# A three-stage kernel on one core: a new written-out order of all steps, other engines for many small steps, and three hand-overs that wait for all readers

## The chip, the cores and the metric

The kernel runs on one NeuronCore of a Trainium2 chip. The metric is the device time of one execution in microseconds (us). The program uses five engines side by side: TensorE (PE, matrix products into PSUM), VectorE (DVE), ScalarE (ACT), GpSimd (POOL, which doesn't reach PSUM here), and SyncE (SP), whose queue issues most transfers. Each engine runs its own list of instructions strictly in order and waits on semaphores for the others.

## The reference, cut to what matters

Three layers follow each other, on 4 batches of 768 positions and 320 channels, all in f32:

```
for t in range(768):                       # mLSTM, 8 heads of 40
    m_new = maximum(f[t] + m, i[t]);  f_s = exp(f[t] + m - m_new);  i_s = exp(i[t] - m_new)
    C = f_s * C + i_s * outer(v[t], k[t]);  n = f_s * n + i_s * k[t]
    y[t] = sigmoid(o[t]) * (C @ q[t]) / maximum(abs(n @ q[t]), 1)

h = relu(x @ w_in);  u, v = h[:, :512], h[:, 512:]       # gMLP
v_n = (v - mean(v)) / sqrt(var(v) + 1e-6)
x = (u * (w_spatial @ v_n + b_spatial)) @ w_out

for e in range(4):                         # attention experts, two of four chosen per position
    a = softmax(causal(0.125 * (x @ wq[e]) @ (x @ wk[e]).T))
    out += chosen_weight(e) * (a @ (x @ wv[e])) @ wo[e]
```

## The kernel before, in words

Each batch is cut into 6 blocks of 128 positions, 24 blocks n in all; gMLP and the q/k/v products work on units of up to 3 blocks (9 units). Precision comes from splitting: a f32 operand becomes a high f16 half (a cast, on ACT, DVE or POOL) and a low half (operand less high half, one subtraction with two inputs on DVE or POOL), and a product is made of three f16 products. Only the first 6 blocks (NF=6) multiply decay weights and values in f32.

The mLSTM is computed block by block. Names in the order are thread names with a number. PL loads q/k, v/o gates and the gate rows (SP). PD and FH make the decay matrix (PE, then exp on ACT, then a causal mask on POOL). PM and FS scale q/k and split them into stacks `qs` (strings qks, qkh, qkl), transposed by a DMA on SP into `qkT`. FW multiplies q by k and by the decay. PV and FP split the values (wf, wh, wl, vh, vl). FM updates the state and splits it (cm, ch, cl). PM goes on with the numerator, the division and the gate (exd, y), splits the result (x1h, x1l) and transposes it into `x1T`. PN normalises a block for the gMLP, with a power of -0.5 on POOL; PU and FG are the gMLP; PQ, FQ, FV and FO make q, k, v and the choice of experts; PA, FE and FZ are attention, where rows `ahl` are transposed by SP into `aT` and results `os` into `oT`, and PA stores them (string res casts the result out of PSUM). PI, PS, PW, PO and PR load and split the weights (PS the spatial ones), their loads issued from ACT's queue; PG and FT prepare the gates, FU sends their rounded pieces to DRAM.

Each thread is a Python generator that yields between steps: the engine of its next step, the buffers it needs, and the events it waits for. `ORDER` (line 348) is a written-out list of thread names, 3,108 of them: `Flow.run` (line 292) takes one name after the other and lets that thread do its next step. So the list fixes the order of instructions on every engine. `CFG` (line 312) holds a string per kind of step, one letter per instance (a ACT, v DVE, p POOL, - none). `_cost` (line 44) and `charge` keep bookkeeping times; they matter here only in that a buffer is taken in the order of the times at which its copies came free (`buffers`, line 265). All matmul and vector calls pass through one helper (line 145), hence L145 in nearly every row of the profile.

Hand-overs that the change touches: in `gates` (from line 560) a f32 tile is rounded to three bf16 pieces in turn, pieces 0 and 2 sharing a buffer, and `send` (line 631) copies each to DRAM; in `mlstm` the step x1l ends with the return of the block's v/o buffer; in `gmlp` the last unit of a batch returns the batch's normalised tiles.

Of the kernel before, what the change touches and what calls it, by code (L numbers as in the profile page):

```python
# [363 lines left out]
PV4 PV5 PM4 PM3 PK3 PN2 PM3 PV4 PT5 PL5 PM3 PV5 PN2 PK3 PM3 PN2 PN2 PM3 PM3 PN2 FM5 FM4 PM3 PN2 PN2 PD5 FH10 FH11 PM4
FH10 FM4 PM3 PD5 PU0 FH11 PM4 PK4 FH10 PN2 PL6 FH11 FM4 PM4 PM6 PN2 FM4 PM6 FW10 FS12 FW11 PM4 FM4 PK4 PU0 FG0 FS13
FW11 FW10 PN3 FG0 PM4 PK4 PT6 PL6 PV6 PM4 PT6 FS13 PM5 PV6 FP6 PM4 FS12 PN3 PM4 PM4 PN3 FP6 PM6 PN3 PM4 PN3 PN3 PD6
FH12 PV6 PN3 FG0 PN3 PM5 PV6 FH12 FG0 PM4 PN3 FH13 FH12 PM5 FG0 FH13 PL7 PD6 PN3 FW12 FH13 FG1 FW12 PM5 PV6 FW12 FW13
PM5 PN4 FG1 PM5 FW12 PM5 FW13 PM5 FW13 PL7 PM7 FM6 FR6 PN4 PM7 PM5 FW13 FG2 PM5 FM6 FS15 PM5 PN4 PN4 PM6 FM6 FG2 FG3
PM5 PN4 PM6 FS15 FS14 FM6 PN4 PT7 PL7 FG1 PM6 PV7 FS14 PU0 FG2 PV7 FP7 PM6 FG1 PN4 PT7 PM7 PN4 FP7 PM6 FG3 PD7 FH14
FH15 PX0 PX0 PM6 FH14 FG2 PV7 FH15 PD7 PN5 PN4 FH14 PV7 PN4 FH15 PL8 PV7 FG3 PM6 PN5 PU1 FG2 PN5 FG3 PN5 PM6 PM6 FM7  # L370
PM6 PN5 FW14 FW15 FW14 FG3 FM7 PM6 FG2 FW15 FW14 FG3 PN5 FM7 FW15 FG2 FW14 PM8 PL8 FM7 PM8 FG3 FS17 FW15 FG1 FM7 FS16
PM7 PN5 FS17 PN5 PN6 FR7 FS16 PM8 PN5 PN5 PM7 PT8 FG2 PN6 PM7 FG3 PT8 FG2 PV8 FG0 PN6 PM7 FG2 PN6 PL8 FG3 PV8 FP8 FG1
PM7 PL9 FG3 FG2 FG0 PM7 PN6 FG3 FG2 PM7 FG1 FP8 PD8 FH16 FH17 PN6 FH16 FG1 FG3 FH17 PD8 FG0 PM7 PN6 PN6 FG1 FG4 FG1
FH17 PM7 PM7 PN6 FH16 FG1 FG0 FG1 PM7 FG5 PN6 PM9 FG0 PM7 PV8 PM9 FW16 FG4 FW17 FG5 FS19 FW16 FG6 FG0 PL9 FW17 PV8
FS18 FG0 PV8 FW16 FG7 FW17 FG6 FS18 FW16 FM8 FW17 PU1 PN7 PU0 FG7 FM8 FR8 FS19 PT9 PL9 PV9 PT9 FM8 PM9 PU0 PM8 PV9 FM8
PN7 PD9 FH18 FM8 FH19 PM8 FH18 PN7 PD9 FG6 FH19 PM8 FH18 PN7 FH19 FP9 PL10 PM8 PN7 PM8 PN7 PM8 PM8 FP9 PN7 PM8 PN7
FW18 FW19 FG6 PV9 PN7 FG7 FW18 PM8 FW19 FW18 PM8 PN7 PV9 FW19 PM10 PV9 FW18 FW19 FM9 PM8 PM9 PM10 FS20 FS21 FS21 PM8
# [1139 lines left out]
```

## Time and profile before

| | |
|---|---|
| median of 3 runs (lowest to highest) | 592.48 us (589.35 to 596.07) |
| the profiled execution: span from its first to its last instruction | 589.3 us; the fastest of the runs took 589.35 us |
| instructions | 14241 |
| mean granted TensorE clock | 0.984 of full speed |

The profile is of one execution. A busy share is an average over stages with different limits, and an idle engine costs nothing unless what it does next is waited for. PE's ends are modelled, so its busy time is an upper bound of its work. In the chain of waits, time is put down to an engine only while the chain ran through it; "DMA" there is a transfer that was waited for.

### The profile page before, as it was taken

Reading aid. Unit: us, or ns where it says so; the run is one execution under the profiler, and the core shown is the slowest. Engines: PE = TensorE matmul, PEld = TensorE weight load, DVE = VectorE, ACT = ScalarE, POOL = GpSimd, SP = SyncE. Lnnn points to the kernel's source line nnn. Section 1 sums busy time; section 2 is a strip of 40 time slices with the busy share of each in tenths; the row PEclk is TensorE's granted clock in tenths of the full one; section 3 lists DMA queues with packets and bytes.
Section 4 is the critical chain, followed back from the end, with each engine's and each line's share of the span. In section 5 each row is a group of like instructions: output and inputs, shape, how many; then the busy total and the mean of one; then the engine's idle time right before and its main releaser. Section 6 shows DMA issues by size and latency. Waiting matters only on the chain.

```text
span 589.3 us, 14241 instructions
## 1 busy us (share of the span) xinstructions
PE 484.1 (82%) x5384; PEld 344.4 (58%) x5384; DVE 483.2 (82%) x1253; ACT 345.3 (59%) x823; POOL 183.1 (31%) x306
## 2 busy tenths in 40 slices
PE   1104588899989888999989998999898999987984
PEld 0004556555646547576665665666475768776773
DVE  7899977868887788989899877999987886658883
ACT  3454446677555587657757447763737643217785
POOL 3022557575564134333324552244310000000000
PEclk9999999999997999999999998999999999999999
DMA  6768583545452879969679687548865855346820
GB/s 191 201 210 203 123 197 72 129 83 112 76 135 58 170 156 177 178 127 151 143 172 186 114 183 132 126 65 158 141 131 128 161 121 85 80 101 116 163 66 23
DMA packets 179404, 78.73 MB, mean 134 GB/s; under 512 B 160198, under 2 KB 168456, under 8 KB 179336
## 3 DMA queue, kind: packets, MB, share of 16 engines
q1 hardware_dynamic: 173552, 69.04, 59.2%
q10 hardware_dynamic: 5784, 8.79, 5.1%
q8 instruction: 42, 0.69, 0.5%
q14 instruction: 26, 0.21, 0.1%
HBM read 25.31 MB, written 4.52 MB: 51 GB/s over the span
## 4 chain that ended last, share of the span: by engine, by line
PE 32%; DVE 28%; DMA 15%; ACT 11%; issue 6%; POOL 5%; SPq 3%; ACTq 0%; DVEq 0%; POOLq 0%
PE g L145 30%; SPq L145 3%; DMA rows<-r_dram 3%; DVE ahl L145 3%; DVE sm L145 3%; DVE g L145 3%; DMA oT<-os 3%; DMA aT<-ahl 2%; PE pst L145 2%; DMA qkT<-qs 2%; ACT pst L145 2%; DVE qs L145 2%; DVE u L145 2%; DVE aT L145 2%; ACT ahl L145 2%
## 5 line engine op out<-in xcount | busy, mean ns | idle before, releaser
L145 PE MATMUL g<-wsT,vn 128*128 128x384 f16 (+2 forms) x612 | 93.4, 307 | 0.1
L145 PEld LDWEIGHTS <-vn 128*128 128x128 f16 x648 | 59.7, 98 | 31.4 <-issue 0.6
L145 PEld LDWEIGHTS <-qkst 128*128 128x128 f16 x424 | 35.5, 100 | 28.1 <-issue 9.3
L145 PE MATMUL g<-gT,w_h 128*128 128x384 f16 (+2 forms) x288 | 49.1, 315 | 2.1 <-DVE ahl L145 2.1
L145 ACT ACTIVATE pst<-pst,sm 128x640 f32<-128x640 f32 (+1 forms) x32 | 26.5, 830 | 37.5 <-DVE sm L145 37.5
L145 PE MATMUL g<-qkst 128*128 128x384 f16 (+4 forms) x224 | 37.7, 298 | 8.8 <-DVE ahl L145 5.6
L145 POOL TENSOR_SCALAR_AFFINE_SELECT dd<-dd 128x512 f32<-128x512 f32 x48 | 31.0, 666 | 44.6 <-ACT dd L145 44.5
L145 ACT ACTIVATE dd<-g 128x512 f32<-128x512 f32 x48 | 26.3, 598 | 20.4 <-PE g L145 20.3
L145 PEld LDWEIGHTS <-w_h 128*128 128x128 f16 x288 | 27.2, 100 | 16.8 <-issue 3.9
L145 ACT ACTIVATE g<-g,sm 128x256 f32<-128x256 f32 (+3 forms) x64 | 32.4, 510 | 6.5 <-DVE sm L145 6.1
L145 PE MATMUL g<-vv,aT 128*128 128x64 f16 x1008 | 33.8, 193 | 2.8 <-DVE sm L145 0.9
L145 PE MATMUL g<-wi_h,x1T 128*128 128x512 f16 x120 | 31.7, 397 | 4.0 <-DMA x1T<-xs 2.0
L145 PEld LDWEIGHTS <-aT 128*128 128x128 f16 x1008 | 32.2, 98 | 4.8 <-issue 3.0
L145 DVE TENSOR_REDUCE sm<-g 128x1 f32<-128x256 f32 (+3 forms) x64 | 29.0, 479 | 5.7 <-PE g L145 5.5
L145 PE MATMUL g<-x1T,wi_h 128*128 128x384 f16 (+2 forms) x180 | 31.9, 308 | 1.5 <-DVE ahl L145 0.8
L145 DVE TENSOR_TENSOR ahl<-pst,ahl 128x640 f16<-128x640 f32 (+1 forms) x32 | 28.3, 883 | 5.6 <-ACT ahl L145 5.0
L145 PEld LDWEIGHTS <-x1T 128*128 128x128 f16 x192 | 18.3, 100 | 24.9 <-issue 4.2
L145 PEld LDWEIGHTS <-qkT 80*128 80x128 f16 (+1 forms) x512 | 24.2, 100 | 12.9 <-DMA qkT<-qs 6.7
L145 DVE TENSOR_REDUCE sm<-pst 128x1 f32<-128x640 f32 (+1 forms) x32 | 28.2, 882 | 3.5 <-PE pst L145 3.2
L145 POOL TENSOR_TENSOR nt<-nt,mhalf 128x1 f32<-128x1 f32 x24 | 15.4, 642 | 49.5 <-DVE nt L145 38.6
L145 DVE TENSOR_TENSOR ahl<-g,ahl 128x128 f16<-128x128 f32 (+3 forms) x64 | 29.4, 480 | 1.5 <-ACT ahl L145 1.4
L145 PE MATMUL g<-rows 96*128 96x128 bf16 x192 | 17.3, 238 | 15.8 <-DMA rows<-r_dram 12.0
(241 smaller groups left out, 1362.7 us busy)
## 6 DMA issues: line engine op xcount, KB each, us to landing
vo<-in_qkvo_dram SPq DMA_DIRECT2D x22, 324.0 KB
qkf<-in_qkvo_dram SPq DMA_DIRECT2D x21, 320.0 KB
qkst<-qkh SPq DMA_DIRECT2D x14, 288.0 KB
out_dram<-res SPq DMA_DIRECT2D x24, 160.0 KB
vn<-in_w_in_dram ACTq DMA_DIRECT2D x12, 256.0 KB
qkst<-qkh SPq DMA_DIRECT2D x16, 192.0 KB
vn<-in_w_sp_dram ACTq DMA_DIRECT2D x12, 192.0 KB
vn<-in_w_out_dram ACTq DMA_DIRECT2D x6, 256.0 KB
```

Of the source, the lines that this page charges most:

```text
L145: r = f(*args, **kw)
```

## The change

All 3,108 names of ORDER are put in a new order, and four steps without instructions (PU) are added. 28 strings of CFG, four letters of `th` and one of `to` are rewritten. In the bookkeeping, a transfer is counted with 1500 ns and 600 bytes per ns of landing time, where it was 600 ns and 240, a f32 product with 5 ns on top, where it was 200, and a forked thread starts no earlier than the end of what its parent has issued. Three yields wait for more: the third rounding of the gates for the sending of the first piece (its event also gets a name of its own), x1l for the split of the weighted values, and the return of the normalised tiles for the gated products of all units of the batch. Lines of further strings and of the order are left out below.

```diff
--- before.py
+++ after.py
@@ -49,13 +49,13 @@
         return 1200.0 + 225.0 * max(0.0, n - 8.0), 1090.0 - 26.0 * n, (900.0, 180.0 * n + 40.0), False
     if op == "dma_start":
         o = kw.get("out", args[0] if args else None)
-        return 335.0 if lane == "act" else 550.0, 600.0 + o.nbytes() / 240.0, (600.0, 40.0 + max(60.0, o.nbytes() / 290.0)), False
+        return 335.0 if lane == "act" else 550.0, 1500.0 + o.nbytes() / 600.0, (600.0, 40.0 + max(60.0, o.nbytes() / 290.0)), False
     o, i = args[0], args[1] if len(args) > 1 else args[0]
     if lane == "pe":
         n = o.free_size()
         if i.dtype == F32:
             t = 4 * max(n, 128)
-            return t / 2.4 + 200.0, LAT[lane], (t / 1.2, 4 * n), False
+            return t / 2.4 + 5.0, LAT[lane], (t / 1.2, 4 * n), False
         if i.free_size() == 64:
             return n / 4.8 + 17.0, LAT[lane], (n / 2.4 + 10.0, n / 2), False
         return max(25.0, n / 2.35 + 3.0), LAT[lane], (max(25.0, n / 1.2), n), False
@@ -242,7 +242,7 @@
 
     def fork(self, gen, kind, x):
 
-        self.start(gen, kind, x, self.cur.t, self.cur.lent)
+        self.start(gen, kind, x, max(self.cur.t, self.cur.end), self.cur.lent)
 
     def pick(self, what, x):
 
@@ -310,166 +310,168 @@
     qkh=1, qkst=1, vv=9, ahl=3, aT=5, num=1, res=2, os=1, oT=2, g=4, s=2, sm=4, vx=2, wx=1, ld=3)
 
 CFG = dict(
...
-    qkl="vvvpvvvvvvvpvvvpvvpvvpvvpvpvvpvpvpvppvvvvvvvvvpp",
...
-    wl="pvvpv-vvppp-vvvvv-ppvvv",
...
-    cl="vpvvv-vvvvv-vvvpv-vpvvv",
...
-    vl="------vpvpvppvvvvvvpvvvv",
...
-    res="vvvaavvvavvaaaavvvaaavva",
...
+    qkl="ppvvpvpvpvpvpvpvpvvpvppvppppppvppvpvpppppppppppv",
...
+    wl="vvvpv-pvppp-ppppp-vppvp",
...
+    cl="ppppv-ppppv-ppvpp-ppppp",
...
+    vl="------ppppppppppppppvvvv",
...
+    res="aavaaaavvaaavaaaaaaaavaa",
     th=(
         "--------------------------------------------------------------------------------------------------------"
-        "------------------------------------------------------------------------aaaavaaaaaaaaaaa"
+        "------------------------------------------------------------------------aaaaaaavaaavaava"
     ),
-    to="----------------------va",
+    to="----------------------aa",
 )
 TIM = dict(NF=6, NP=2, NX=21, last=(0, 1, 2, 3, 4, 5), units=((3, 3), (3, 3), (3, 3), (3, 2, 1)))
 ORDER = """
-PX1 PX2 PR0 PG0 PG1 PL0 PX3 PR0 PI0 PI4 PX3 PG0 PI1 PW1 PW0 PW2 PO0 PO2 PO1 PR0 PG0 PG1 PG0 PG1 PL0 PM0 PM0 FS0 PG0
...
-FS2 PS0 PS5 PS4 PS5 PL2 PS0 PS4 PS1 FS3 PS1 FT1 FM0 FS3 PO0 FW0 PM1 FW1 PS5 FM0 PO0 FW0 FM0 FW1 PM2 PS4 FM0 PM0 PL2
...
-FE94 FE95 PA22 FE94 PA23 FE95 FZ95 FZ95 PA22 PA23 PA23 PA23 FZ95 FE95 FE94 PA23 FE95 FE94 PA23 FE95 FE95 PA23 PA23
-PA23 PA23 PA23 PA23 PA23 PA23 PA23
+PG1 PX1 PX3 PG1 PX2 PO1 PW1 PO2 PW2 PO0 PG0 PL0 PR0 PG0 PS1 PI5 PG1 PG0 PM0 PG1 PR0 PG1 PG0 PO2 PM0 FS0 FS0 PL0 PG0
+PI1 PG1 PG0 PG1 PI2 PG0 PI5 PO1 PG0 FT0 PG0 PX3 PW0 PO2 PI4 PO0 PG0 FU0 PI5 PG1 FT1 PI2 PV0 PG0 PI5 PG0 FS1 PW0 PI0
+PI5 PO2 FU1 PI4 PG0 PX3 FU2 PG0 PW1 PI4 PG0 PG0 PO0 PW2 PI4 FT0 PI2 PL0 PD0 FH0 FH1 FS1 PG0 PD0 PI1 PI3 PV0 PG0 PV0
+PX0 PL1 PO1 PM0 PO0 FH0 PL2 PO0 PV0 FM0 PI3 PO2 PI1 PL1 PG1 PM1 PW2 PI0 FH0 PS5 PS1 FM0 FW0 PI2 PI1 FH1 PG1 PW2 PS4
...
+FE93 PA23 PA22 FE94 FZ95 PA21 FE94 FE95 FZ95 FE94 PA23 FE95 FE95 PA23 PA23 PA23 PA23 PA22 PA23 PA23 PA23 PA22 PA22
+PA23 PA23 FR22
 """
 
 
@@ -605,10 +607,10 @@
         flow.signal("gw", j)
         flow.fork(columns(j, ft, mm), "FT", j)
         for x in range(3):
-            yield dve
+            yield dve, *[("a", j, x - 2)] * (x > 1)
             p = pcs[:, 2 * (x % 2):2 * (x % 2) + 2]
             dve.tensor_copy(p, am)
-            flow.signal("pc", j, x)
+            flow.signal("pcs", j, x)
             if x < 2:
                 yield dve
                 dve.tensor_tensor(am, am, p, op=ALU.subtract)
@@ -629,7 +631,7 @@
         flow.done("aT", "aT")
 
     def send(j, x, p):
-        yield sp, ("pc", j, x), ("rd", 0)
+        yield sp, ("pcs", j, x), ("rd", 0)
         for y in range(2):
             sp.dma_start(r_dram[3 * y + x, 2 * j:2 * j + 2, :, :, y].rearrange("b h c s -> (b h c) s"), p[:, y])
         flow.signal("a", j, x)
@@ -1065,7 +1067,7 @@
         x = ex.rearrange("p h d -> p (h d)")
         yield on("x1h", n)
         on("x1h", n).cast(xs[:, 0:DM], x)
-        yield on("x1l", n)
+        yield on("x1l", n), *[("w", n)] * (c < NC - 1)
         on("x1l", n).tensor_tensor(xs[:, DM:DM + 64], x[:, 256:320], xs[:, 256:320], op=ALU.subtract)
         on("x1l", n).tensor_tensor(xs[:, DM + 64:2 * DM], x[:, 0:256], xs[:, 0:256], op=ALU.subtract)
         flow.done(m["own_vo"])
@@ -1180,6 +1182,7 @@
             flow.done("s", "g", "g")
         yield pe, *[("gj", m, j) for j in range(4)]
         if c0 + gs == NC:
+            yield pe, *[("gj", x, j) for x in range(m) if units[x][0] == b for j in range(4)]
             flow.done(*[vn.pop(b * NC + t)[1] for t in range(NC)])
         x2[m] = gT, flow.take("gT")
         flow.signal("x2", m)
```

## Rows read from the trace of the kernel before

**Rows 1.** The page's span and busy time of each engine, with its share and instructions.

```profile
span 589.3 us, 14241 instructions
PE 484.1 (82%) x5384; PEld 344.4 (58%) x5384; DVE 483.2 (82%) x1253; ACT 345.3 (59%) x823; POOL 183.1 (31%) x306
```

**Rows 2.** The page's chain that ended last: shares by engine, and by line.

```profile
PE 32%; DVE 28%; DMA 15%; ACT 11%; issue 6%; POOL 5%; SPq 3%; ACTq 0%; DVEq 0%; POOLq 0%
PE g L145 30%; SPq L145 3%; DMA rows<-r_dram 3%; DVE ahl L145 3%; DVE sm L145 3%; DVE g L145 3%; DMA oT<-os 3%; DMA aT<-ahl 2%; PE pst L145 2%; DMA qkT<-qs 2%; ACT pst L145 2%; DVE qs L145 2%; DVE u L145 2%; DVE aT L145 2%; ACT ahl L145 2%
```

**Rows 3.** Stages: length; busy PE, PEld, DVE, ACT, POOL; clock, DMA share, GB/s.

```profile
0.00:105.00 105.00, 47.80 (x438) 36.58 (x439) 88.64 (x228) 50.60 (x110) 42.86 (x78) 1.00 0.67 170
105.00:200.00 95.00, 87.74 (x884) 57.17 (x883) 75.42 (x184) 58.19 (x125) 49.01 (x80) 0.96 0.53 107
200.00:340.00 140.00, 126.54 (x1472) 87.43 (x1471) 122.56 (x329) 94.96 (x243) 54.00 (x86) 0.99 0.83 157
340.00:472.00 132.00, 122.39 (x1340) 83.91 (x1339) 115.04 (x294) 81.77 (x200) 36.75 (x61) 0.99 0.70 135
472.00:564.00 92.00, 84.54 (x1003) 67.17 (x1001) 67.78 (x189) 41.95 (x116) 0.50 (x2) 0.98 0.55 109
564.00:590.00 26.00, 15.14 (x261) 12.14 (x259) 13.78 (x36) 17.83 (x32) 0.00 (x0) 0.95 0.12 39
```

**Rows 4.** Timeline, first gates: start, length, instruction, idle time and releaser.

```profile
19.56 0.29 DVE L145 CAST aT<-aT 96x256 bf16<-96x256 f32 x1 [0.27 <-DMA r_dram<-aT]
```

**Rows 5.** Waits: who waited for whom, total us, times, longest.

```profile
POOL dd L145 <- ACT dd L145: 44.5, 17, 20.3
POOL nt L145 <- DVE nt L145: 38.6, 8, 25.7
...
PE g L145 <- DVE ahl L145: 12.4, 17, 1.5
...
PE g L145 <- DMA oT<-os: 4.5, 4, 2.6
```

**Rows 6.** Groups by form (count, busy us, mean ns, idle before): low halves, both engines.

```profile
L145 DVE TENSOR_TENSOR qs<-qkf,qs 128x320 f16<-128x320 f32 x30 | 17.1, 579 | 3.2 <-ACT qs L145 3.1
...
L145 DVE TENSOR_TENSOR cs<-cf,cs 80x328 f16<-80x328 f32 x17 | 11.0, 649 | 1.2 <-ACT cs L145 1.1
...
L145 POOL TENSOR_TENSOR qs<-qkf,qs 128x320 f16<-128x320 f32 x12 | 9.5, 791 | 12.2 <-ACT qs L145 7.4 <-DVE sm L145 3.9 <-ACT vv L145 0.7
...
L145 DVE TENSOR_TENSOR vx<-vo,vx 128x328 f16<-128x328 f32 x13 | 7.4, 570 | 0.1
...
L145 DVE TENSOR_TENSOR wx<-vo,wx 128x328 f16<-128x328 f32 x10 | 5.4, 539 | 0.5 <-ACT wx L145 0.5
...
L145 POOL TENSOR_TENSOR vx<-vo,vx 128x328 f16<-128x328 f32 x5 | 4.6, 919 | 3.5 <-DVE vx L145 3.4
...
L145 POOL TENSOR_TENSOR wx<-vo,wx 128x328 f16<-128x328 f32 x5 | 4.0, 810 | 1.5 <-ACT wx L145 0.8 <-DVE wx L145 0.6
...
L145 POOL TENSOR_TENSOR cs<-cf,cs 80x328 f16<-80x328 f32 x3 | 2.4, 806 | 3.5 <-DVE cs L145 3.4
```

**Rows 7.** Tiles cs and qs: ns shortest/median/longest, first and last start.

```profile
L145 DVE TENSOR_TENSOR cs<-cf,cs x17: 483/495/1647, 56.0 to 415.7; 80x328 f16<-80x328 f32 x17
...
L145 DVE TENSOR_TENSOR qs<-qkf,qs x30: 440/482/1025, 45.7 to 394.2; 128x320 f16<-128x320 f32 x30
...
L145 POOL TENSOR_TENSOR qs<-qkf,qs x12: 787/790/794, 121.2 to 421.9; 128x320 f16<-128x320 f32 x12
```

**Rows 8.** Tile qkT: the products of q and k, first and last start.

```profile
L145 PE MATMUL g<-qkT x192: 216/219/314, 54.1 to 428.7; 120*128 120x128 f16 x192
```

**Rows 9.** Groups by form: the low half of a spatial weight piece.

```profile
L145 DVE SCALAR_TENSOR_TENSOR wsT<-vn,wsT 128x384 f16<-128x384 f32 x12 | 6.1, 546 | 0.0
```

**Rows 10.** Groups by form: POOL's causal masks, and its powers for the norm.

```profile
L145 POOL TENSOR_SCALAR_AFFINE_SELECT dd<-dd 128x512 f32<-128x512 f32 x48 | 31.0, 666 | 44.6 <-ACT dd L145 44.5
...
L145 POOL TENSOR_TENSOR nt<-nt,mhalf 128x1 f32<-128x1 f32 x24 | 15.4, 642 | 49.5 <-DVE nt L145 38.6 <-DVE den L145 10.8
```

More of the change, by code (lines that the diff above doesn't have):

```diff
@@ L339 @@
-    osh="aaaaaaaaaaaavaavvvvvaaaa",
-    res="vvvaavvvavvaaaavvvaaavva",
+    vs="aaaaaaaaaaaapppaaappappp",
+    qks="aaaaaaapaapvappaapppppva",
+    qkh="aaaaaaaaaaaaaavaavpvappvpapvpaaapapappaapapvappv",
+    qkl="ppvvpvpvpvpvpvpvpvvpvppvppppppvppvpvpppppppppppv",
+    e1="aaaaaapapapappvpvppaaapp",
+    wf="vvpvp-ppvvv-ppppv-vpppp",
+    wh="aaaaa-appaa-ppvav-pvaaa",
+    wl="vvvpv-pvppp-ppppp-vppvp",
+    ch="aaaap-ppvva-ppapp-paapp",
+    cl="ppppv-ppppv-ppvpp-ppppp",
+    cm="-vpvp--ppvp--pvpp--pppp",
@@ new lines @@
+    exd="pvvpppvvppppppvppvppvvpp",
+    y="vvvvppvpvppppppppvppppvp",
+    x1h="aaavaaappvpapavpppppvpvp",
+    x1l="vvpvpvvpvppppppppppppppp",
+    w2="aaaaaaaa",
+    vnh="aavavvavvaaaavaaavaaaava",
+    ru="vaaaaaaaaavvvaaavaavaaavaaaaavaaaaaa",
+    vh="------aapapppppaaaapvvap",
+    vl="------ppppppppppppppvvvv",
+    Wh="------------avaaavvaaaaaaaaavavvaavaaaaaaaaaaaaa",
+    gh="aaavaaaavaaaaavavvaaaaaaaavvaaavavaa",
+    qh="avaaaaaavvaavvaavaaaaavavvvaaavaaaaa",
+    vvh="avaaaaaaaaavvvvvvaaavaaa",
@@ L364 @@
[L364 to L377, printed above, removed]
-FR9 FG6 FG5 FS20 FM9 PL10 FG6 PM10 FG6 FM9 FM9 PM9 FM9 PN8 PM9 PL11 PT10 PV10 PM9 PM9 PL10 FG7 PM9 PT10 FG5 PN8 PM9
@@ new lines @@
+PI1 PG1 PG0 PG1 PI2 PG0 PI5 PO1 PG0 FT0 PG0 PX3 PW0 PO2 PI4 PO0 PG0 FU0 PI5 PG1 FT1 PI2 PV0 PG0 PI5 PG0 FS1 PW0 PI0
+PI5 PO2 FU1 PI4 PG0 PX3 FU2 PG0 PW1 PI4 PG0 PG0 PO0 PW2 PI4 FT0 PI2 PL0 PD0 FH0 FH1 FS1 PG0 PD0 PI1 PI3 PV0 PG0 PV0
+PX0 PL1 PO1 PM0 PO0 FH0 PL2 PO0 PV0 FM0 PI3 PO2 PI1 PL1 PG1 PM1 PW2 PI0 FH0 PS5 PS1 FM0 FW0 PI2 PI1 FH1 PG1 PW2 PS4
+PI3 PM1 FS3 FS2 FS2 PL2 PR0 PT0 FS3 FH1 PI0 FW1 PV1 PL1 PD1 PV1 PI4 FM0 PW1 PM1 PI0 PW0 PI3 PW1 PV1 PV1 PM2 PT0 FH2
+PW0 FH3 PD1 FH2 FM1 PS0 PI5 FH3 PT2 PM2 FW1 FH2 FW0 PL3 FH3 FW2 PT1 FW3 PW0 PI3 PI4 FS4 FS4 FW2 FM1 PM0 FM0 PI0 PL2
@@ new lines @@
+PW0 FH6 PN0 FM3 PW2 PS3 PN0 FS9 PR0 PD4 FH8 PG1 FH9 FH7 PD4 PM2 PN1 FS10 PG1 PT3 PK0 PK1 PV4 PN0 PM2 PN1 FH9 FH8 PS2
+PM2 PI1 PM4 PR0 PV4 PS0 PM2 PN0 PK1 PK2 FS11 PK0 PM2 PK1 FM2 PN1 PM2 FW6 FW7 FM2 PK0 PK3 PL6 FW6 FW7 PK2 FM3 PM3 PS2
+PI1 PN0 PN1 PM2 PS0 PN0 PK2 PL5 FM4 PM3 FS10 FS11 PM2 PI2 FH8 PN0 PN1 PK3 PN0 FW8 PT3 PS2 PK3 PI0 PM3 PS1 FM4 PN1
+PK4 FH9 FW9 PM6 PM3 FW8 PM3 PM3 PS4 PL5 PV5 PD5 FM3 FW9 PN2 PM3 PM6 FS13 FM4 PM3 PM3 PM3 PN1 FS12 PM4 PM3 PT5 PM5
+FH10 PN1 PI1 PM4 PU0 FS13 PN1 FH11 PN2 PD5 PM4 PU0 FS12 FH10 PN2 PM4 PS4 FH10 FW10 PM4 FM4 FH11 FG0 PM4 FW10 PL6 PN2
@@ new lines @@
+FH11 PN2 PK4 PM4 FG0 PM3 PN3 PT6 FM5 PN2 PN2 PV6 PS5 FW11 PK4 PM4 PT6 PN2 PM4 PV5 FW11 PS1 PN3 PV6 PM6 PL7 PL6 PD6
+PS1 PN3 FM4 FG0 PN2 PS5 FP6 PM4 PT5 PM5 PM5 PM4 PM7 PM7 PN2 PR0 PN3 FG1 FG0 PN3 PN3 PL7 FS15 FP6 FG1 PM5 PN3 PS2 PR0
+FH12 FH13 PS4 FH12 FH12 PS3 PM4 FH13 PM5 FS14 FG2 FG1 FS15 PM5 PN3 FW12 FH13 PN3 FS14 FG2 FW12 PM5 FW12 PN3 FG3 PV6
+FW13 FW13 FR6 FW13 PD6 PL7 PD7 FW13 PM5 PM7 FG0 FW12 PV7 PN4 PS3 FG3 PM5 PV6 FH14 FH15 FG3 PT7 PM5 PD7 PM6 PV6 PM5
+PS3 PM5 PM6 FH14 FM6 FG1 FH15 FG3 PV7 FH14 PL8 PS5 PN4 PT7 PM6 PN4 FG2 PN4 PM6 PM5 FM6 FW14 PM6 FH15 FW15 FP7 PM6
@@ new lines @@
+PN4 PM6 FG3 FG2 FP7 FW14 PM6 PM6 FW14 PM6 PL8 FW15 PM8 PN4 PM8 FM6 FS16 FS17 PN5 FG3 FG0 FG1 PU1 PN5 FS17 PN4 FW14
+FM6 FG2 PV7 FG1 FW15 FS16 PN4 FW15 PM6 PM7 PV7 PN4 PN5 PN4 FG2 PV8 PV7 PN5 PT8 PM7 FG3 PX0 PN5 PL8 FM7 FG2 PM7 PN5
+PM7 FM7 PN5 PD8 FH16 FH17 FH16 FM7 FG1 PR0 PS5 FH16 PD8 FG0 PN5 PM7 PM8 FH17 PL9 PN5 PN6 FW16 PM7 PN5 FH17 FW17 FG0
+FG3 PM7 FG2 FG3 FG1 FG2 PM7 FW17 PT8 PV8 FG4 FW16 FR8 PM9 PN6 FM7 PM9 FW17 PM7 FW16 PM7 FM7 FG3 FW17 FG4 PN6 FG3 PM7
+PL9 FP8 FG1 FR7 FG5 FG2 FG6 FG1 PN6 FS19 FS18 PM7 PN6 FW16 FG1 PN6 FG3 PU0 FP8 FG6 FG1 PV8 FG7 PU1 FG5 PM8 FG0 FS18
@@ new lines @@
+FG0 PR0 PM8 PM8 PL9 PD9 FG7 FG2 FS19 PM9 PN7 FG2 PV8 PL10 FG0 FG0 PU0 PV9 PV8 PN6 PM8 FM8 FM8 PN6 FH18 FH19 PD9 FH18
+PN7 PM8 FG6 FH19 PM8 PM8 PM8 PN7 PT9 FH18 FM8 PM8 PM8 PU0 PV9 PN6 FM8 FW18 PM8 FW18 PN7 PL10 FW18 FP9 FH19 PM10 FP9
+FG7 FW19 FG6 PV9 PN7 PM10 FW18 PN6 PN7 FG7 FG7 FW19 FS21 FR9 PV9 FU5 PV9 FG6 FG5 FS20 PR0 FG7 FW19 FS20 FG6 FM8 FW19
+PL10 PD10 FG6 PT9 PM9 FG5 FH20 PM8 FG7 PM9 FS21 FH20 PN7 PN7 FU4 FG5 FM9 PM9 PK5 FH21 FG5 PV10 FM9 PM9 FG5 PM10 PL11
+PT10 FM9 PN7 FH20 FH21 PV10 FP10 FP10 FG4 FH21 PD10 PM9 PM9 PV10 FW20 FW21 PN7 PX0 FW20 FW20 PK6 PT10 FW21 FR10 PM9
```

228 lines of the change are left out of this document (101 added, 127 removed).

## The prediction

> **What bounds the kernel now.** I read the page first. PE and DVE are each busy 82% of the span, ACT 59%, POOL 31% [rows 1]: no engine is saturated over the whole, so the order and the hand-overs between engines count as much as any load. The chain of waits says the same: it runs through PE for 32% of the span, DVE 28%, DMA landings 15%, ACT 11%, POOL 5% [rows 2]. Cut into stages [rows 3], the kernel has three faces. Up to 105 us (weights split, first mLSTM blocks) DVE works 88.6 us and PE only 47.8: DVE and the chains through it set this stage. From 105 to 564 us PE is busy 421.2 of 459 us and DVE 380.8: PE nearly full, DVE a close second, with 37.8 us of PE idle left. The last 26 us belong to ACT (17.8 us).
>
> **The three new waits, the longer landing time, the shorter f32 product and the later start of forked steps** issue no instruction. They act when an order is searched for; in the program that is built they only shift the bookkeeping times by which a free copy of a buffer is picked. For the gates the wait exists already: the third rounding on DVE sits 0.27 us behind the send that reads the buffer it overwrites [rows 4]. Behind it on DVE all of DVE's queue waits, and still it is 0.27 us. The other two waits only hold a buffer's return. I take nothing for all of them. A differently picked copy could save or cost at most what PE now waits for DVE to free or fill its banks, 12.4 us [rows 5]; the value nearest to the 0.27 us is zero.
>
> **Engine choices.** I compared the strings letter by letter and priced each letter with its engine's mean. Four families carry the shift from DVE to POOL. The q/k low halves (qkl): 25 leave DVE, 7 come back, net 18 x 0.579 = 10.4 us less on DVE, 18 x 0.791 = 14.2 more on POOL. The state's low half (cl): 14 x 0.649 = 9.1 less, 14 x 0.806 = 11.3 more. vl: 9 x 0.570 = 5.1 less, 9 x 0.919 = 8.3 more. wl: net 6, 3.2 less and 4.9 more [rows 6]. Together DVE loses 27.8 us and POOL gains 38.7. The remaining strings trade some 260 instructions both ways and nearly cancel; with them the whole is DVE -33, POOL +44, ACT +0.5 us. A shorter DVE pays only where DVE is on the chain: 28% of 589.3 is 165 us of its 483.2 busy, 34%, so -33 x 0.34 = -11 us (bounds: 0, if PE hides it all, and -33). POOL is on the chain for 5%, 29.5 of 183.1 us, 16%: +44 x 0.16 = +7 us (bounds 0 and +44). What hides the rest of POOL's growth is its idle time, some 289 us of the first 472 [rows 3]; if that cover went, the +44 would show.
>
> These moves have a cost that the trace shows in DVE's own rows. The state's low half takes 0.483 us at best, 0.495 in the middle and 1.647 at worst, the q/k low half 0.440, 0.482 and 1.025, while the same q/k work on POOL hardly varies (0.787 to 0.794) [rows 7]: now and then DVE is held up, POOL is not. Mean less minimum is 17 x 0.166 + 30 x 0.139 = 7.0 us. After the change 3 and 16 or so of these 47 stay on DVE, so at a POOL load 227/183 as high the hold-ups come to about 3.5 us. The Trainium skill (SBUF — State Buffer, Who interferes with whom) speaks against such a move: DVE's second port pair belongs to GpSimd too, as an exclusive lock, and whichever comes second stands still for the whole instruction. By that rule longer POOL instructions could take back what DVE gains; this is a rival below. The trace agrees that some DVE instructions wait for about one POOL instruction.
>
> **The start.** The old order puts 140 weight and gate steps ahead of the first mLSTM product of q and k (FW0), which starts at 54.1 us [rows 8]; the new one only 54, and FW0 stands at place 109 instead of 218. But PE being early is not the point, since DVE sets this stage: ahead of the first gMLP product (FG0) stand 167 such steps before and 147 after. Of the 20 put off, 11 are the spatial weights, a third of them on DVE at 0.546 us [rows 9]: about 2 us leave the stage and come back later beside PE. The first stage has 16.4 us without DVE work [rows 3], which work of four mLSTM blocks could fill; bounds -16 and +2. I take -2, nearest to the row of the weights. The loads of the weights put off are issued from ACT's queue, now behind more of ACT's work; what hides that is that the spatial products need them only after 105 us, and ACT has half of the first stage free (50.6 of 105 us).
>
> **Transfers.** In the order I counted PE's work (by output columns, all products making PE's 484.1 us) between the last instruction that writes a tile and the product that reads its transposed copy. For the attention rows (aT) the smallest cover rises from 2.0 to 4.2 us and the median from 6.7 to 8.6; for oT the median goes from 4.8 to 9.8; x1T 4.8 to 6.3; qkT falls from 9.2 to 8.6. SP keeps every one of its transfers; new is only where each stands in its queue, and an early output store behind a late result can hold those behind it. Landings of oT and aT make 3% and 2% of the chain [rows 2], but PE's own wait for oT is 4.5 us [rows 5]. Bounds: -28 (both gone) and +5 (qkT worse); I take -3, near PE's own row.
>
> **Hand-overs.** Of some 1,500 steps that follow a step of the same thread on another compute engine, 1,021 had under 1 us of other work on their engine in between, now 774, 24% fewer. If PE's idle 37.8 us shrank alike, that were -9; the DVE term counts part of this already, so I take half, -4.5 (bounds 0 and -38).
>
> **Sum.** -11 + 7 - 2 - 3 - 4.5 = -13.5 us, on the profiled 589.3: 575.8. That execution is the fastest of the three shown (589.35 to 596.07, median 592.48), 3.1 us under the median, so in terms of a median **579 us**.
>
> **Rivals.** *PE is the bound.* From 105 us PE is 92% busy; a DVE that idles more then buys nothing. The -11 and the -4.5 go, +7 - 2 - 3 = +2 stays: 591 us profiled, 594 as a median. For: PE makes 32% of the chain, 30 of it in products into the g banks [rows 2]. Against: DVE is on the chain almost as long. Chance 0.13. *The shared pair takes the relief back:* every moved subtraction holds what DVE needs 0.2 us longer than DVE did; the -11 is gone, the sum is -2.5, 587 us profiled, 590 as a median. The rule cited above is this one; the shrinking number of exposed DVE instructions speaks against it. Chance 0.07.
>
> *Slower: POOL becomes late.* 48 masks and 24 powers on POOL gate a PE product or the norm's DVE step [rows 10]. Today POOL waits for them, 44.5 and 38.6 us in all [rows 5], so they run at once. If half of the 72 find a moved subtraction just begun, that is 36 x 0.79 = 28 us, half of it on the chain: +14, 603 us profiled, 606 as a median. It decides once POOL's idle time ahead of masks and powers has gone to a third. Against: POOL would still be idle for half of the first 472 us. Chance 0.17.
>
> *More than the sum:* the start's idle DVE filled and both transfers covered, 562 us. Chance 0.10. *That the change does nothing* applies to its bookkeeping lines alone; order and strings are read directly by the code that emits.
>
> **Chances.** Forecast (568 to 586) 0.53, more 0.10, the two rivals of no change 0.20, slower 0.17. What a measurement here tells from no change is about 1%, 5.9 us. Faster by more than that: 0.53 + 0.10 = 0.63; within it 0.20; slower 0.17. The range runs from 560, under the larger gain, to 599, over the no-change rivals; most of the slower rival is what it leaves out.
>
> **What would show it.** On the new page: DVE near 450 us, POOL near 227, ACT unchanged; the first q-k product well before 54 us with little gain by the end of that stage; q/k and state low halves on DVE closer to their minima; PE's wait for oT under 2 us; less PE idle between 105 and 564 us. POOL's idle time ahead of masks and powers should stay the larger part. I am wrong if PE's idle time in the middle grows (a late POOL or a transfer held in SP's queue would be named by PE's waits), or if DVE's busy time doesn't fall by about 30 us.

## The result, and the profile after

The changed kernel takes **544.48 us** (median of 4 runs, 540.96 to 546.25) against 593.4 us for the kernel before in the same session: a ratio of **0.918** (95% interval 0.913 to 0.923), 49 us less. The forecast was 579, the range 560 to 599: the direction was right and the gain three and a half times too small. Executions more than 1.5% above the fastest of the same kernel are left out of the ratios but not of the medians, which without them would be 593.7 us for the run mirrored, 569.7 for mirror_mlstm and 546.9 for old_code.

The page after answers to [rows 1, 2]: span, busy time of each engine, chain by engine and by line.

```profile
span 542.0 us, 14223 instructions
PE 477.9 (88%) x5384; PEld 342.3 (63%) x5384; DVE 464.4 (86%) x1195; ACT 343.8 (63%) x823; POOL 223.5 (41%) x364
PE 45%; DVE 15%; DMA 9%; ACT 8%; issue 5%; POOL 4%; SPq 2%; ACTq 0%; POOLq 0%; DVEq 0%
PE g L145 42%; DMA aT<-ahl 4%; PE pst L145 3%; DVE ahl L145 2%; SPq L145 2%; ACT ahl L145 2%; DMA x1T<-xs 2%; DVE sm L145 1%; ACT g L145 1%; DMA oT<-os 1%; DVE g L145 1%; ACT pst L145 1%; DVE vn L145 1%; DVE num L145 1%; DMA qkf<-in_qkvo_dram 1%
```

POOL does 40.4 us more and DVE 18.8 less, but the span is 47.3 us shorter. DVE's share of the chain falls from 28% to 15%, that of DMA from 15% to 9%, and PE's rises from 32% to 45%: the chain now stays on PE for longer.

The next rows cut the kernel after into the stages of [rows 3], each bound put where the same step of the list stands (columns as there).

```profile
0.00:87.00 87.00, 49.84 (x440) 37.29 (x441) 81.78 (x217) 54.88 (x121) 31.31 (x58) 0.98 0.82 197
87.00:175.00 88.00, 85.17 (x872) 55.52 (x872) 77.10 (x180) 56.19 (x127) 61.11 (x92) 0.98 0.57 121
175.00:306.00 131.00, 121.51 (x1434) 84.83 (x1433) 116.20 (x303) 89.80 (x227) 74.32 (x122) 1.00 0.83 163
306.00:433.00 127.00, 121.83 (x1370) 84.56 (x1368) 109.27 (x275) 81.20 (x195) 55.75 (x90) 1.00 0.73 142
433.00:516.00 83.00, 80.62 (x941) 64.61 (x940) 62.63 (x182) 41.78 (x115) 0.77 (x3) 1.00 0.63 121
516.00:542.00 26.00, 18.92 (x333) 15.49 (x332) 17.39 (x44) 19.91 (x40) 0.21 (x1) 1.00 0.20 61
```

The stages lose 18, 7, 9, 5, 9 and 0 us. In the first, DVE's time without work falls from 16.4 to 5.2 us (87.00 - 81.78) and its work by 6.9. In the four middle ones PE's idle time falls from 37.8 to 19.9 us. So the start gave 18 us, and the other 30 came a few at a time from everywhere but the tail.

Of these 30 us, 17.9 are PE's idle time. The other 12.1 are products: 5.8 us of them now run in the first stage and the tail, and 6.2 are gone, since the same 5,384 products take 477.9 us instead of 484.1. An estimate puts some 5 of the 6.2 down to TensorE's granted clock. In the stretches that the trace gives at the lower level (0.50, which is 1.2 GHz), PE is busy 16.2 us before and 6.5 after; the five products wi_h,x1T took 2.32 us in such a stretch (64.9 us of the trace after) and 1.25 at full clock (81.6 us), so that about half of the difference of 9.7 us is lost to the clock. The prediction has no term for this.

The first and last product of q and k, and of the spatial weights, in the kernel after (ns shortest/median/longest, first to last start), and the low halves that answer to [rows 7]:

```profile
L145 PE MATMUL g<-qkT x192: 216/218/314, 26.0 to 392.8; 120*128 120x128 f16 x192
L145 PE MATMUL g<-wsT,vn x612: 219/326/337, 104.6 to 498.5; 128*128 128x384 f16 x117, 128*128 128x256 f16 x18, 128*128 128x128 f16 x18
...
L145 DVE TENSOR_TENSOR cs<-cf,cs x3: 482/484/730, 92.5 to 259.6; 80x328 f16<-80x328 f32 x3
...
L145 DVE TENSOR_TENSOR qs<-qkf,qs x12: 479/486/1604, 39.8 to 378.3; 128x320 f16<-128x320 f32 x12
...
L145 POOL TENSOR_TENSOR qs<-qkf,qs x30: 781/792/1212, 6.5 to 376.3; 128x320 f16<-128x320 f32 x30
```

The waits that answer to [rows 5] (total us, times, longest):

```profile
POOL dd L145 <- ACT dd L145: 40.1, 19, 9.3
...
POOL nt L145 <- DVE nt L145: 19.6, 10, 4.8
...
POOL nt L145 <- DVE sm L145: 17.7, 2, 15.6
...
PE g L145 <- ACT aT L145: 8.8, 7, 4.2
...
PE g L145 <- DMA rows<-r_dram: 7.9, 2, 4.6
...
PE g L145 <- DVE ahl L145: 3.8, 5, 1.5
```

PE's wait for the low half of the attention rows (ahl) falls from 12.4 to 3.8 us, and POOL still waits for its masks and powers instead of making others wait.

### The profile page after: what moved, and what is told of

It reads as the page before. It is cut to its first block, busy times and chain, and to the rows that moved or that the text cites. A ratio compares the mean times of both kernels' runs of the same rounds, so it can differ in the third digit from the quotient of the medians.

```text
span 542.0 us, 14223 instructions
## 1 busy us (share of the span) xinstructions
PE 477.9 (88%) x5384; PEld 342.3 (63%) x5384; DVE 464.4 (86%) x1195; ACT 343.8 (63%) x823; POOL 223.5 (41%) x364
## 4 chain that ended last, share of the span: by engine, by line
PE 45%; DVE 15%; DMA 9%; ACT 8%; issue 5%; POOL 4%; SPq 2%; ACTq 0%; POOLq 0%; DVEq 0%
PE g L145 42%; DMA aT<-ahl 4%; PE pst L145 3%; DVE ahl L145 2%; SPq L145 2%; ACT ahl L145 2%; DMA x1T<-xs 2%; DVE sm L145 1%; ACT g L145 1%; DMA oT<-os 1%; DVE g L145 1%; ACT pst L145 1%; DVE vn L145 1%; DVE num L145 1%; DMA qkf<-in_qkvo_dram 1%
## 5 line engine op out<-in xcount | busy, mean ns | idle before, releaser
L145 POOL TENSOR_SCALAR_AFFINE_SELECT dd<-dd 128x512 f32<-128x512 f32 x48 | 33.5, 704 | 40.3 <-ACT dd L145 40.1
L145 PE MATMUL g<-gT,w_h 128*128 128x384 f16 (+2 forms) x288 | 47.6, 308 | 0.0
L145 ACT ACTIVATE dd<-g 128x512 f32<-128x512 f32 x48 | 27.9, 594 | 23.1 <-PE g L145 23.1
L145 POOL TENSOR_TENSOR df<-lg 128x48 f32<-128x48 f32 (+2 forms) x8 | 2.0, 254 | 93.0 <-DVE lg L145 81.2
L145 DVE TENSOR_REDUCE sm<-g 128x1 f32<-128x128 f32 (+3 forms) x64 | 29.8, 483 | 6.6 <-PE g L145 6.3
L145 PEld LDWEIGHTS <-x1T 128*128 128x128 f16 x192 | 18.4, 102 | 25.5 <-issue 4.8
L145 POOL TENSOR_TENSOR qs<-qkf,qs 128x320 f16<-128x320 f32 x30 | 24.9, 833 | 17.2 <-ACT qs L145 16.2
```

What stands on the lines that cost most here:

```text
L145: r = f(*args, **kw)
```

## The experiments

Ratios are against the kernel before, run beside each. The changed kernel's is 0.918 (0.913 to 0.923).

| run | what it is | median us | ratio (95%) |
|---|---|---|---|
| order_only | new order, old letters | 603.6 | 1.017 (1.009 to 1.025) |
| engines_only | old order, new letters | 611.1 | 1.031 (1.023 to 1.039) |
| early_start | old kernel, new order up to FG0 | 590.3 | 0.998 (0.994 to 1.002) |
| late_start | new kernel, old order up to FG0 | 558.1 | 0.942 (0.935 to 0.948) |
| mirrored | new kernel, letters reversed in quarters | 594.6 | 1.003 (0.998 to 1.007) |
| low_back | new kernel, four old strings | 556.2 | 0.942 (0.938 to 0.947) |
| old_books | new kernel, old bookkeeping | 548.9 | 0.927 (0.919 to 0.934) |
| new_start | early_start with new letters there | 583.7 | 0.989 (0.983 to 0.996) |
| mirror_mlstm | mirrored, mLSTM strings alone | 570.1 | 0.958 (0.953 to 0.964) |
| mirror_late | mirrored, the other strings alone | 569.5 | 0.963 (0.959 to 0.966) |
| mirror_before | old kernel, its letters reversed | 608.3 | 1.027 (1.023 to 1.031) |
| old_code | old code, new order and letters | 547.5 | 0.921 (0.917 to 0.925) |
| neighbours | new kernel, letters traded with the next | 575.1 | 0.971 (0.968 to 0.975) |

**Order and letters apart.** Theory: one of the two carries the gain. Rival: they fit only each other.

```diff
 order_only:    after.py with
-CFG = (after)
+CFG = (before)
 engines_only:  before.py with
-CFG = (before)
+CFG = (after)
```

order_only: 

> The changed kernel with all its code and its new order, but with the old engine strings (CFG of before). Theory 1, the order carries the gain: about 40 of the 48 us stay, 549 to 560 us; the first q-k product still starts near 26 us and DVE busy is back near 483 us. Theory 2, the relief of DVE carries it: the 18.8 us that DVE's busy time fell by come back on PE's path, and more is lost to waits, 570 us or more. Theory 3, order and strings fit only each other: 585 us or more.

engines_only: 

> The kernel before with its old order and code, but with the new engine strings. Theory 1 (the order carries the gain): 585 to 595 us, no more than 1% off the kernel before, although DVE's busy time falls by about 19 us and POOL's rises by about 40. Theory 2 (relief of DVE): 570 to 578 us, as the prediction's -11 and -4.5 would have it or more. Theory 3 (they fit only each other): slower than before, 600 us or more, with PE waiting for work that moved to POOL.

Each half makes the kernel slower, by 1.7% and by 3.1%; together they make it 8.2% faster. Busy times, order_only first, then engines_only:

```profile
span 597.5 us, 14214 instructions
PE 494.0 (83%) x5384; PEld 346.5 (58%) x5384; DVE 485.5 (81%) x1253; ACT 344.6 (58%) x823; POOL 183.8 (31%) x306
```

```profile
span 607.4 us, 14238 instructions
PE 488.3 (80%) x5384; PEld 345.2 (57%) x5384; DVE 465.9 (77%) x1195; ACT 346.4 (57%) x823; POOL 220.1 (36%) x364
```

engines_only has the changed kernel's load (DVE 465.9, POOL 220.1) and is 67 us slower than it: DVE is relieved and merely idles. Theory 3 holds; neither part has a worth of its own that could be added up.

**The same load, other instances.** mirrored separates fit from load: the order stays, and each engine keeps its count of every kind in every quarter. mirror_mlstm and mirror_late do it to two groups of strings (150 and 108 letters; in some strings the quarters are cut at other places than in mirrored, so the letters are not all the same), mirror_before does it to the old kernel, and neighbours trades letters only between instances next to each other.

```diff
 mirrored (one of its strings; after.py)
-    gh="aaavaaaavaaaaavavvaaaaaaaavvaaavavaa",
+    gh="vaaaavaaavvavaaaaavaaaaaaaaaavavaaav",
 neighbours (one of its strings; after.py)
-    vs="aaaaaaaaaaaapppaaappappp",
+    vs="aaaaaaaaaaaappapaapppapp",
```

mirrored: 

> The changed kernel with its order and code; inside each string of engine letters the letters of each quarter (mostly one batch) stand in reverse, 262 letters in all, so that every engine keeps exactly the changed kernel's number of instructions of each kind in each quarter (DVE 1190, POOL 349, ACT 678 by the builder's count), but another block's instance gets them. Theory of fit (each letter belongs to a place in the list): old letters on the new order cost 59 us for 352 letters, so about 44 us for 262 here, 575 to 600 us, with DVE's busy time still near 464. Theory of load (the time follows from how much each engine has): 544 to 552 us.

mirror_mlstm: 

> The changed kernel with letters reversed within quarters, as in the run mirrored, but only in the strings of the mLSTM and of the weighted values (150 letters). Mirroring 262 letters cost 50 us at equal load. If every letter costs alike: +29, 573 us. If these letters hardly matter since the products of gMLP and attention wait for others: 550 us or less. If they carry nearly all of it: 585 us or more.

mirror_late: 

> The changed kernel with letters reversed within quarters only in the strings of the norm, the gMLP, q/k/v and attention (vnh, ru, Wh, gh, qh, vvh, ah, osh, res: ACT or DVE alone, 108 letters). If every letter costs alike: +21, 565 us. If these carry nearly all of the 50 us, since they free the PSUM banks that TensorE writes: 585 us or more. If few misplaced letters are caught by the slack of the list: under 555 us.

mirror_before: 

> The kernel before with its own letters reversed within quarters (292 letters, loads per quarter unchanged). Theory A, the change is a list and strings that fit each other more closely than the old pair: the old pair loses clearly less than the 50 us of the new one, 600 to 625 us. Theory B, both pairs fit equally well: 643 us or so, 50 to 56 us more. Theory C, the old pair doesn't fit at all: 590 to 598 us.

neighbours: 

> The changed kernel with letters traded only between neighbouring instances (0 with 1, 2 with 3, ...: the two halves of one block, or two blocks that follow each other), 248 letters. Reversal inside a quarter left open whether a letter must fit its place in the list or whether it is enough that the load of each engine is right over some 10 to 20 us; here that load stays. Theory of place: as many letters off as in the run mirrored, so about the same loss, 580 us or more. Theory of local load: 556 us or less.

Here are two lines of mirrored's page, which is of its fastest execution (586.1 us):

```profile
span 584.1 us, 14219 instructions
PE 486.8 (83%) x5384; PEld 344.5 (59%) x5384; DVE 468.0 (80%) x1195; ACT 339.7 (58%) x823; POOL 225.4 (39%) x364
```

And its longest wait of PE for DVE (total us, times, longest):

```profile
PE g L145 <- DVE ahl L145: 16.9, 15, 3.6
```

DVE, ACT and POOL have the changed kernel's load to within 4.1 us, and the whole gain is gone. PE waits for the low half of the rows 16.9 us, where it waited 3.8; this one wait is 13 us of the loss, and the rows here do not show what makes up the rest. Theory of load falls. The two halves cost 4.0 and 4.4 points of the ratio (25.6 and 25.0 us), both together 8.5 (50.1 us): the losses add, as far as the two groups make up mirrored. The old pair loses 16 us by the same treatment, with more letters (292 against 262): Theory A, the new list and its letters fit more closely. neighbours came out between its two forecasts: 31 us are lost although each engine's load over a few blocks stays, so most of the fit is one of place in the list; the 19 us up to mirrored may be load over longer stretches, or the other choice of letters.

**The low halves.** low_back puts the four strings of the prediction's main term back.

```diff
 after.py with the strings of before
-    qkl, cl, vl, wl (after)
+    qkl, cl, vl, wl (before)
```

> The changed kernel with four of its strings set back, the low halves qkl, cl, vl and wl, which carry most of the shift from DVE to POOL (65 letters; DVE +28, POOL -39 us of instruction time). Theory of load, with the prediction's shares: +28 x 0.34 - 39 x 0.16 = +3 us, up to +9.5 if POOL was never in the way, 546 to 555 us. Theory of fit alone, 65 of 352 letters of the 59 us: +11, 553 to 558 us. If DVE now binds at nearly every place of the new order, the whole +28 shows, 570 us or more.

It costs 11.7 us by the medians, the value of the theory of fit, just above the upper end of the load's; by the ratios, which compare with the kernel before on the same chip, it costs 2.4 points, 14 us. The run can't say how much of it is load. Its page gives the real size of the load:

```profile
PE 483.2 (87%) x5384; PEld 344.0 (62%) x5384; DVE 477.7 (86%) x1242; ACT 344.6 (62%) x823; POOL 191.5 (35%) x317
```

The four strings put 47 instructions back on DVE, and its busy time rises by 13.3 us (464.4 to 477.7), where the prediction and the expectation have 28; POOL's falls by 32.0, where they have 39.

**The start.** Theory: it is worth the 18 us seen at the first spatial product. Rival: the prediction's 2.

```diff
 early_start: ORDER of before, its first 488 steps sorted as in after
 late_start:  ORDER of after, its first 455 steps sorted as in before
 new_start:   early_start, and the 48 letters these steps read that differ: before -> after
```

early_start: 

> The kernel before with its old engine strings; its first 488 steps (all ahead of the first gMLP product, FG0) stand in the order that the new list gives these steps, the other 2,620 in the old order. Theory 1a, the start is worth what the profile shows at the first gMLP product (105.4 us before, 87.0 after) and the rest of the order keeps it: 574 to 579 us, FG0 near 90 us. Rival, the prediction's term (DVE sets this stage and PE's early work only waits): 588 to 593 us, FG0 at 103 us or later. Second rival, FG0 comes early but the old order gives it back at a later transfer or unit: FG0 near 90 us, time above 585 us.

late_start: 

> The changed kernel with its new engine strings; its first 455 steps (all ahead of FG0) stand in the order that the old list gives them, the rest in the new order. Theory 1a: the 18 us at FG0 are lost and nothing else, 558 to 565 us. Rival (the start is worth 2 us): 545 to 548 us. If more than 25 us are lost, the later order depends on what the start has prepared.

new_start: 

> The kernel before with its first 488 steps in the new list's order, as in the run early_start, and now also the new letters for all engine choices that those 488 steps make (48 letters differ). Theory of fit: the first gMLP product comes at 87 to 92 us, as in the changed kernel (98.1 with the old letters). Then, if the old rest keeps its own fit, it keeps the gain too: 575 to 580 us; if the later old order was fitted to times of the old start, the gain is gone by the end, 586 us or more, as with the old letters.

The first spatial product in the kernel before, then the two products in early_start, then in late_start:

```profile
L145 PE MATMUL g<-wsT,vn x612: 219/326/494, 122.8 to 535.5; 128*128 128x384 f16 x117, 128*128 128x256 f16 x18, 128*128 128x128 f16 x18
```

```profile
L145 PE MATMUL g<-wsT,vn x612: 219/326/328, 124.6 to 534.0; 128*128 128x384 f16 x117, 128*128 128x256 f16 x18, 128*128 128x128 f16 x18
L145 PE MATMUL g<-qkT x192: 216/219/314, 25.5 to 425.7; 120*128 120x128 f16 x192
```

```profile
L145 PE MATMUL g<-wsT,vn x612: 219/326/336, 120.0 to 512.0; 128*128 128x384 f16 x117, 128*128 128x256 f16 x18, 128*128 128x128 f16 x18
L145 PE MATMUL g<-qkT x192: 216/218/314, 52.8 to 406.2; 120*128 120x128 f16 x192
```

In the old list the early first product (25.5 us) buys nothing: the first spatial product comes at 124.6, no sooner than before (122.8), and the time stays the same. The trace shows where the lead goes. Here is the stretch from 93 to 117 us in the kernel before and in early_start (columns as in [rows 3]), then two of PE's rows in early_start, the first of them FG0:

```profile
93.00:117.00 24.00, 19.23 (x210) 13.91 (x209) 19.17 (x49) 15.22 (x31) 14.19 (x24) 1.00 0.57 123
```

```profile
93.00:117.00 24.00, 14.46 (x74) 9.14 (x72) 14.12 (x30) 10.93 (x24) 6.79 (x12) 0.51 0.47 113
...
98.11 1.76 PE L145 MATMUL g<-x1T,wi_h 128*128 128x384 f16 x5 [4.91 <-DVE vn L145]
...
105.45 2.29 PE L145 MATMUL g<-wi_h,x1T 128*128 128x512 f16 x5 [4.63 <-DVE dd L145]
```

FG0 comes 7 us earlier than in the kernel before (98.1 for 105.4), not the expected 15. PE waits 4.9 us for DVE ahead of it and 4.6 us behind it, and the granted clock, which fell when PE had just run out of work (at 93 us), stays at its lower level up to 117 us: the five products of the last row take 2.29 us, in the kernel before 1.24. Over the whole execution PE is busy 491.5 us for 484.1, and the mean granted clock is 0.957 to 0.975 in the ten executions of early_start, against 0.963 to 0.991 in those of the kernel before beside them.

In the new list the old start delays the first spatial product from 104.6 to 120.0, and 13.6 us are left at the end. With its own letters the early start gives the old kernel 1.1%; the expected 87 to 92 us for FG0 were missed, it came at 97.9, behind a wait of 5.4 us for DVE and again with the clock at 0.50 (93 to 106 us). So the start's 14 to 18 us are shown only ahead of the new rest. Whether the old rest would keep an early start whose clock doesn't fall, no run shows.

**Bookkeeping and waits.** old_books and old_code leave every engine's list of instructions as it is and change only which buffer copy a step takes; old_code also leaves the three waits out.

```diff
 old_books (the fork likewise)
-        return ..., 1500.0 + o.nbytes() / 600.0, ...
+        return ..., 600.0 + o.nbytes() / 240.0, ...
 old_code: before.py with ORDER (less four PU steps) and CFG of after
```

old_books: 

> The changed kernel with the three bookkeeping edits taken back (landing time of a transfer, length of a f32 product, start of a forked step); order, strings and waits stay, and so every engine's list of instructions; only which copy of a buffer a step takes can differ. The prediction's term of zero: 542 to 547 us. Rival, the picks carry part of the gain: 550 us or more.

old_code: 

> New order (without its four empty PU steps) and new strings on the code before: none of the three waits, old bookkeeping. Every engine's list of instructions is the changed kernel's; only buffer copies can differ. The prediction's term of zero for all these edits: 542 to 548 us. Rival: the picks or waits carry part of the gain, 551 us or more.

old_books' median of 548.9 lies between its two forecasts; its interval overlaps that of the changed kernel, and old_code, which undoes still more, has 0.921 in more executions. The edits are worth nothing that could be told from zero; at most some 0.8% is open.

**One letter.** How does a misplaced letter cost time? One profile each, with the unchanged kernel run again for the spread.

```diff
 one_letter (after.py)
-    ah, instance 19: a
+    ah, instance 19: v
 five_letters: vnh 0, ah 19, qh 14: a -> v; ah 50, qh 25: v -> a
```

one_letter: 

> The changed kernel with a single letter turned: the cast ahl<-pst of attention step FE19 (0.70 us on ACT at 224.2 us of the changed kernel's trace) stands on DVE, at the same place of the list. In the run mirror_late, where this letter is turned among 107 others, the cast took 0.82 us on DVE, a 4-element DVE step behind it took 1.92 us in place of 0.16 while POOL ran three instructions without a pause, and TensorE then waited 2.16 us for the low half of the rows. If a single misplaced letter does this by itself: DVE's subtraction ahl<-pst comes 0.8 to 2.6 us later against its neighbours and TensorE shows a new wait of about 2 us near 227 us. If it takes the whole disturbance of many letters: no wait over 0.5 us there. Whole time within 1% of the changed kernel either way.

five_letters: 

> The changed kernel with five single letters turned, far apart in time: vnh 0 (ACT to DVE, 76 us), ah 19 (ACT to DVE, 224 us), qh 14 (ACT to DVE, 308 us), ah 50 (DVE to ACT, 410 us), qh 25 (DVE to ACT, 471 us). Theory of fit, with 50 us for 262 letters: 0.2 us a letter on average, about 1 us in all, uneven: most letters nothing, some a wait of 1 to 2 us on TensorE. Rival, each letter costs its own length or more: 4 us or more.

after_again: 

> The changed kernel unchanged, for how far two executions' instructions lie apart: less than 0.5 us around any place, and 540 to 547 us in all.

First the changed kernel's timeline at that place (start, length, instruction, idle time before): DVE, POOL, PE.

```profile
224.24 0.70 DVE L145 SCALAR_TENSOR_TENSOR g<-g,dd 128x512 f32<-128x512 f32 x1 [0.17 <-PE g L145]
224.85 0.16 DVE L145 TENSOR_SCALAR sm<-sm 128x4 f32<-128x4 f32 x1
...
225.95 0.81 DVE L145 TENSOR_TENSOR ahl<-pst,ahl 128x640 f16<-128x640 f32 x1
...
225.33 0.93 POOL L145 TENSOR_TENSOR xs<-vo,xs 128x64 f16<-128x64 f32 x2
226.73 0.79 POOL L145 TENSOR_TENSOR qs<-qkf,qs 128x320 f16<-128x320 f32 x1 [0.46 <-ACT qs L145]
...
223.97 3.09 PE L145 MATMUL g<-wsT,vn 128*128 128x384 f16 x18
226.90 0.82 PE L145 MATMUL pst<-qkst 128*128 128x384 f16 x6
```

The same place with the one letter turned:

```profile
224.84 0.83 DVE L145 CAST ahl<-pst 128x640 f16<-128x640 f32 x1
225.59 0.69 DVE L145 SCALAR_TENSOR_TENSOR g<-g,dd 128x512 f32<-128x512 f32 x1
226.18 1.90 DVE L145 TENSOR_SCALAR sm<-sm 128x4 f32<-128x4 f32 x1
...
229.02 0.81 DVE L145 TENSOR_TENSOR ahl<-pst,ahl 128x640 f16<-128x640 f32 x1
...
225.94 0.93 POOL L145 TENSOR_TENSOR xs<-vo,xs 128x64 f16<-128x64 f32 x2
226.83 0.79 POOL L145 TENSOR_TENSOR qs<-qkf,qs 128x320 f16<-128x320 f32 x1
227.59 0.46 POOL L145 TENSOR_SCALAR vx<-vo 128x328 f16<-128x328 f32 x1
...
224.64 3.09 PE L145 MATMUL g<-wsT,vn 128*128 128x384 f16 x18
229.88 0.83 PE L145 MATMUL pst<-qkst 128*128 128x384 f16 x6 [2.15 <-DVE ahl L145]
```

A cast of 0.83 us joins DVE's queue. The step on 4 elements per partition two places behind it, 0.16 us long before, now starts just after POOL has begun xs, and lasts 1.90 us, until POOL's run of four instructions (xs is two) ends. The same step lasts 1.91 us in five_letters and 1.92 in mirror_late, which turn the same letter, and 0.16 in both executions of the unchanged kernel. The low half of the rows, which the step stands ahead of, comes so late that PE waits 2.15 us where it had not waited. Against the changed kernel PE is 0.67 us late ahead of this place (224.64 - 223.97) and 2.98 behind it (229.88 - 226.90): one letter costs 2.3 us. With PE's products matched one by one against the changed kernel's trace, nothing of that came back: they are 2.8 us late at 260, 3.1 at 400 and 3.9 at the end.

In five_letters the same letter costs 2.3 us again, and so does qh 14, where PE waits 2.2 us for DVE (qkh). Behind vnh 0 PE is 0.8 us later, and of the two that leave DVE ah 50 costs under 0.4 and qh 25 1.3. The rest of its lag is not shown to come from the letters: behind vnh 0 it grows by 2 us, and behind qh 14 by 1.5, while the clock is at its lower level (81 to 88 and 320 to 323 us), and 3.4 us arise at 212 us, where the unchanged kernel, run again, shows as much. The whole times say nothing at this size: the unchanged kernel took 550.0 us in its single run here, above the forecast 547, one_letter 547.6 and five_letters 558.4.

## Why the prediction was wrong

**The step that failed** is the one behind the whole sum: order and engine choices were priced as separate terms, each by averages, and added. The engine strings went in as counts times mean durations times a share of the chain, the order as a count of close hand-overs. Neither looks at which instance stands where. Run apart, the two parts cost 1.7% and 3.1%; that alone makes any sum of separate worths wrong. With the fit broken on both sides, mirrored and mirror_before differ by 13.7 us, about the -13.5 forecast; this may be chance, as the letters turned are not the same in number. The fit itself is the rest: the new pair loses 50 us with it, the old pair 16.

**Engine choices (-11 + 7).** POOL's growth was right (+40.4 for +44), DVE's relief was not (-18.8 for -33, DVE near 464 where 450 was named), one of the prediction's own signs of being wrong. Its price of a letter was too high on DVE: the four families come to 13.3 us in low_back, not 27.8. But load is not what the time followed: with DVE at 468.0 and POOL at 225.4, mirrored gains nothing.

**The start (-2, bounds -16 and +2).** Mis-sized: 18 us at the end of the stage, of which 13.6 reach the end. I had seen the 16.4 us without DVE work and took the value nearest to a row that had nothing to do with them, that of the weights put off. That PE's early work is worth nothing of itself holds in early_start, but there two waits for DVE and the lower clock take its lead back.

**Transfers (-3).** The wait for oT has gone from PE's long waits as foretold, and DMA's share of the chain fell by 6 points; PE's wait for the gates' rows went from 12.0 to 7.9 us. No run took this term by itself.

**Hand-overs (-4.5).** Mis-sized, and by a reading that can't see fit. PE's idle time in the middle fell by 17.9 us, not 4.5 to 9. Counted once more in one way for all lists (work by the lengths in `_cost`), steps with under 1 us of other work in between are 1,076 before and 825 after, but also 810 in order_only and 827 in mirrored, which are no faster than the kernel before.

**Bookkeeping and waits (0).** Right, within what old_code and old_books resolve.

**The rivals.** PE as the bound: no, its idle time in the middle halved and its share of the span rose to 88%. POOL late: no, its waits for masks (44.5 to 40.1 us) and for the norm (38.6 to 19.6 + 17.7) remain. The shared port pair: as a whole no. DVE instructions more than 0.3 us above the median of their operation and shape are 44 with 22.9 us in excess before, 45 with 23.6 after, though POOL works 22% longer. (Of the 47 low halves of cs and qs, 15 stay on DVE, not the 19 of the prediction, and only those of the state came closer to their minimum: the longest took 0.730 us where it took 1.647, the longest of q/k 1.604 where it took 1.025.) In one place, behind the one letter, it may have acted: the step of 1.90 us. By the rule of the Trainium skill (SBUF — State Buffer, Who interferes with whom), DVE's second port pair is GpSimd's too, under an exclusive lock; the trace agrees there, with a DVE step that stood still through POOL's instructions. That the lock was the reason isn't shown by itself. The larger gain (562) was priced too low for what it says: with the start at its bound of -16 and the transfers at -28, the prediction's own terms add up to -52.5, 537 us profiled or 540 as a median, and the range would have held the result. That would have been luck, since the order, of which both are parts, gains nothing by itself.

## What to carry to other kernels

When a written-out order and the choice of engines change together, they are one change: price them by single places (what stands ahead of this step on its engine, what runs on POOL at that moment, who waits for the result), not by loads, since a load that the order doesn't use becomes idle time. Where that can't be done, the two parts' terms are no sum, and the range should reach as far as the idle time of the engine on the chain. To find out whether a schedule is closely fitted, trade a few choices at equal load: a loss of 50 us against 16 told the two apart. And before an early start is called worthless, compare the granted clock and the length of one product in that stretch: early_start lost part of its lead there.
